# One row-max entry moves from the second to the third attention burst, and score matmuls and row maxima alternate there

## The chip, the cores and the metric

The kernel runs on one core of a Trainium2 chip. The metric is the device time of one execution in microseconds (us), as the median of several runs. TensorE (PE) multiplies and writes its results into PSUM, which has eight banks of 128 x 512 float32 here; VectorE (DVE) and ScalarE (ACT) read them out of the banks; GpSimd (POOL) works on SBUF; SyncE (SP) and the queues of the other engines issue DMAs.

## What is computed

The input is a sequence of 2048 tokens of width 640. Four layers follow each other, A, B, A, B; each is a layer norm, an attention with 32 heads of width 20, a projection, and a residual sum. Layer A is a linear attention. Layer B cuts the sequence into four segments of 512 tokens; in each segment it adds a causal softmax attention to a read of a memory that the earlier segments have filled:

```
logits = jnp.einsum("bhqd,bhkd->bhqk", qs, ks) * scale + mask
p = _softmax(logits, axis=-1)
a_dot = jnp.einsum("bhqk,bhkd->bhqd", p, vs)
o = g * a_mem + (1.0 - g) * a_dot
```

The softmax needs the maximum of each row of logits before the exponentials are taken. The change touches only the order of work in this softmax attention.

## The kernel before

Everything that is not softmax attention (norms, transposes, projections, linear attention, memory) is called dense work below: it is one stream of steps, written as Python generators. The softmax attention is a second stream. A small planner (`run`) interleaves the two while the program is built, by costs that the steps yield. The order of PE's instructions is the order in which the program is written (`MANUAL = ("PE",)`); the other engines' orders are made by a scheduler when the program is built. Every engine then runs its own list strictly in that order.

Softmax attention works on groups of four heads: 8 groups per segment, 32 per B layer, 64 in all. Each group takes part in three successive rounds, as `new`, `prev` and `old`, and each round has three bursts on PE, the three lists of `STRETCHES`. Between two bursts stands dense work, about one projection step of 15 matmuls (L325 or L311), often with a few transposes (L268). An entry of a burst is (operation, number, age), where age 0 is `new`, 1 is `prev` and 2 is `old`:

- `max` (`row_max`, L687 and L694): PE computes logits with queries on the partitions into two banks (one per head of a pair), and DVE reduces each block to its row maxima, with the mask added. `MAXES` says which blocks: entries 0 and 2 are one block of 512 keys per bank, entries 1 and 3 are 384 + 128, entry 4 is 256 + 256. The four reductions of entry 3 belong to the same group as those of entry 4.
- `split` (L703, L704): DVE turns the group's 16 columns of maxima, `mg`, into two float16 parts, `m`. It needs all five `max` entries of the group.
- `rows` (`max_rows`, L712, L714, L717): PE transposes `m` (L712), ACT copies it, and two DMAs on SP's queue write it as extra rows into the queries' tile `qs`, so that the logits of the next step come out with the maximum subtracted. It is done for `prev` in the first burst of the next round.
- `exp` (`scores`, L729, L733, L740): PE computes logits with keys on the partitions into a bank, ACT takes the exponential (L733), POOL clears the part above the diagonal. Entries 0 to 3 of `EXPS` fill two banks each, so does entry 4.
- `sum` (`weigh`, L756): 32 matmuls that weigh the values. `copy` (L762) takes the result out, `out` (`normalize`, L769 to L782) transposes it on PE and divides on DVE.

In the first burst PE does `exp 4`, `max 0`, `max 1`, then `rows` (L712), then the `sum` entries (L756). L712 stands in front of the 32 L756 and of everything behind them.

All banks come from one pool of eight (`bank`, `bufs=8`). A tile takes the place of an earlier one whose readers are done, as the scheduler sees it when the program is built; on the chip PE then waits at the first matmul into a bank until the last reader of the former tile has ended. Each `max` holds its two banks until DVE has reduced them, each `exp` until ACT has read them.

```
for stretch in STRETCHES:
    for op, k, back in stretch:
        G = (new, prev, old)[back]
        ...
    yield SLOT
```

## Time and profile before

| what | value |
|---|---|
| median of 3 runs | 1830.88 us (1830.0 to 1831.1) |
| profiled execution, its own time | 1833.06 us |
| its span, first to last instruction | 1831.3 us |
| mean granted TensorE clock | 0.995 |
| PE busy | 1713.7 us (94%) |
| DVE busy | 1145.0 us (63%) |
| ACT busy | 911.1 us (50%) |
| POOL busy | 502.5 us (27%) |

A timeline row gives the start, the length, the engine, the source line, the operation, what it writes and reads, the shape, how many equal instructions were merged into the row, and in brackets the idle time before it and what ended that. Matmuls overlap each other, and the length of a matmul row reaches to the modelled end of its last matmul; so the time that PE needs for a piece of work is read from start to start. A row of a table of windows gives the stretch, its length, and the busy time of each engine in it with the number of its instructions. In the table of waits stand the waiting engine, tile and line, who ended the wait, the total in us, how often, and the longest.

Softmax attention lies between about 342 and 975 us and between about 1245 and 1806 us of the span.

### The profile page before, as it was taken

What the parts mean: (1) busy time and instruction counts of PE and PEld (TensorE: products, weight loads), DVE (VectorE), ACT (ScalarE), POOL (GpSimd) and SP (SyncE); (2) the same over time, 40 slices, a digit from 0 to 9 for tenths busy, and PEclk for the clock granted to TensorE, in tenths of its full rate; (3) what the DMA queues carried; (4) which work ended last, traced back from release to release, by engine and by line L of the source; (5) the groups of instructions that cost most, each with busy time, mean ns of one, the idle gap of its engine ahead of it and who ended that gap; (6) DMA issues with size and microseconds to landing.
All of it is one profiled execution on the core that took longest, in us unless ns stands there. A gap on an engine that the chain in (4) does not pass through costs nothing.

```text
span 1831.3 us, 36161 instructions
## 1 busy us (share of the span) xinstructions
PE 1713.7 (94%) x13032; PEld 1070.3 (58%) x13032; DVE 1145.0 (63%) x3890; ACT 911.1 (50%) x1696; POOL 502.5 (27%) x925
## 2 busy tenths in 40 slices
PE   6999999999999999898989999999999989998998
PEld 4666676654664565453556776766546546544555
DVE  7655343677777676766663421527687777777783
ACT  5455433256556545545554433333664665565553
POOL 1534440022122113224344334200221231232231
PEclk9999999999999999999999999999999999999999
DMA  7452443312222332352212112432122222323332
GB/s 254 154 188 92 159 143 99 107 58 93 88 67 86 105 103 76 105 186 71 66 56 87 51 33 91 137 108 99 51 91 92 86 90 91 101 77 100 122 112 87
DMA packets 123307, 185.96 MB, mean 102 GB/s; under 512 B 13676, under 2 KB 85484, under 8 KB 120952
## 3 DMA queue, kind: packets, MB, share of 16 engines
q1 hardware_dynamic: 109416, 137.44, 23.5%
q0 software_dynamic: 4496, 25.23, 3.8%
q10 hardware_dynamic: 9216, 20.98, 3.0%
q8 instruction: 103, 1.69, 0.4%
q14 instruction: 76, 0.62, 0.1%
HBM read 104.41 MB, written 78.64 MB: 100 GB/s over the span
## 4 chain that ended last, share of the span: by engine, by line
PE 75%; DVE 11%; ACT 6%; issue 4%; POOL 2%; DMA 2%; SPq 1%; POOLq 0%; ACTq 0%; DVEq 0%
PE ps L325 33%; PE ps L311 18%; PE ps L756 7%; DVE junk L694 4%; PE ps L268 4%; ACT pe L733 3%; PE ps L370 3%; PE ps L729 3%; PE ps L452 2%; PE ps L687 2%; POOL e L341 1%; PE ps L582 1%; PE ps L769 1%; DVE nat L547 1%; PE ps L574 1%
## 5 line engine op out<-in xcount | busy, mean ns | idle before, releaser
L694 DVE CUSTOM_DVE_ANT_0 junk<-ps,maskw 128x512 bf16<-128x512 f32 (+3 forms) x1024 | 499.5, 488 | 83.2 <-PE ps L687 27.1
L733 ACT ACTIVATE pe<-ps,lsc 128x512 f32<-128x512 f32 x640 | 392.7, 691 | 174.5 <-PE ps L729 171.5
L740 POOL TENSOR_SCALAR_AFFINE_SELECT pe<-pe 128x256 f32<-128x256 f32 (+1 forms) x640 | 233.5, 371 | 677.4 <-ACT pe L733 672.0
L325 PEld LDWEIGHTS <-xT 128*128 128x128 f16 x2880 | 281.7, 99 | 124.1 <-issue 18.6
L325 PEld LDWEIGHTS <-oT 128*128 128x128 f16 x1920 | 187.1, 98 | 79.6 <-issue 7.6
L341 POOL TENSOR_SCALAR e<-e 128x320 f32<-128x320 f32 (+1 forms) x104 | 163.7, 1574 | 163.2 <-ACT e L337 154.4
L756 PE MATMUL ps<-pe,v 128*32 128x512 f32 (+3 forms) x2048 | 155.4, 438 | 13.7 <-ACT pe L733 6.8
L729 PE MATMUL ps<-qs,ks 62*128 62x384 f16 (+3 forms) x1024 | 132.2, 299 | 33.4 <-DVE mg L694 22.4
L325 PE MATMUL ps<-w_Bo,oT 128*128 128x320 f16 x960 | 142.8, 301 | 2.6 <-DVE mg L694 1.4
L325 PE MATMUL ps<-w_Bv,xT 128*128 128x320 f16 x960 | 141.3, 301 | 1.9 <-DVE mg L694 1.9
L325 PE MATMUL ps<-w_Av,xT 128*128 128x320 f16 x960 | 141.2, 305 | 1.6 <-DVE w_Av L234 1.0
L311 PE MATMUL ps<-xT,w_Bq 128*128 128x512 f16 x600 | 139.5, 379 | 1.5 <-DVE mg L694 0.9
L311 PE MATMUL ps<-xT,w_Bk 128*128 128x512 f16 x600 | 139.5, 379 | 0.2 <-DVE xn L391 0.2
L325 PE MATMUL ps<-w_Ao,oT 128*128 128x320 f16 x960 | 139.5, 299 | 0.0
L311 PE MATMUL ps<-xT,w_Aq 128*128 128x512 f16 x600 | 136.0, 379 | 1.3 <-DVE xT L273 0.9
L325 PE MATMUL ps<-w_Ak,xT 128*128 128x320 f16 x960 | 135.6, 299 | 1.4 <-DVE mg L694 1.4
L348 ACT ACTIVATE v<-ps 128x320 f32<-128x320 f32 x128 | 55.4, 436 | 143.2 <-PE ps L325 138.9
L291 POOL TENSOR_TENSOR rs<-rs,mhalf 128x1 f32<-128x1 f32 x64 | 35.3, 551 | 302.6 <-DVE rs L290 302.6
L687 PE MATMUL ps<-ks,qs 60*128 60x512 f16 (+3 forms) x1024 | 108.4, 297 | 5.8 <-ACT pe L733 3.6
L756 PEld LDWEIGHTS ps<-pe,v 128*32 128x32 f32 x2048 | 65.3, 110 | 81.2 <-issue 66.3
L547 DVE SCALAR_TENSOR_TENSOR nat<-ps,nat 128x512 f16<-128x512 f32 x80 | 55.3, 691 | 90.3 <-ACT nat L546 86.4
L546 ACT ACTIVATE nat<-ps 128x512 f16<-128x512 f32 x80 | 48.0, 600 | 105.9 <-PE ps L311 76.3
(151 smaller groups left out, 2240.9 us busy)
## 6 DMA issues: line engine op xcount, KB each, us to landing
x<-xn ACTq DMA_DIRECT2D x48, 320.0 KB
qs<-qd SPq DMA_DIRECT2D x128, 120.0 KB
ks<-kd SPq DMA_DIRECT2D x128, 120.0 KB
xo<-x SPq DMA_DIRECT2D x48, 320.0 KB
pqd<-pq POOLq DMA_DIRECT2D x40, 256.0 KB, 2.5
pqi<-pqd SPq DMA_DIRECT2D x32, 320.0 KB
qd<-nat SPq DMA_DIRECT2D x40, 256.0 KB
kd<-nat SPq DMA_DIRECT2D x40, 256.0 KB
```

What stands on the lines that cost most here:

```text
L268: nc.tensor.transpose(pt[:, (c - c0) * P:(c - c0 + 1) * P], src[:, c * P:(c + 1) * P], self.ident)
L311: nc.tensor.matmul(p, w[:, c, a, t * P:(t + 1) * P], xT[:, c, b, :], start=k == 0, stop=k == 3 * C - 1)
L325: nc.tensor.matmul(p, xT[:, c, a, i * P:(i + 1) * P], w[:, c, b, n * HN:(n + 1) * HN], start=k == 0, stop=k == 3 * C - 1)
L341: nc.gpsimd.tensor_scalar(e, e, 1.0, eps, op0=OP.min, op1=OP.add)
L348: self.nc.scalar.activation(vv[:, n * HB:(n + 1) * HB, :DH], p.rearrange("p (h e) -> p h e", e=DH), AF.Copy, scale=V_SHIFT)
L547: nc.vector.scalar_tensor_tensor(nat[:, 1], p, QK_SHIFT, nat[:, 0], op0=OP.mult, op1=OP.subtract)
L687: nc.tensor.matmul(bs[par][:, a:a + n], qs[r, p, i * P:(i + 1) * P], ks[r, p, :n], start=True, stop=True)
L694: nc.vector.tensor_tensor_reduce(junk[:, :n], bs[par][:, a:a + n], self.maskw[:, SEG - n:], 1.0, NEG, OP.add, OP.max, G["mg"][:, par, p, i ...
L729: nc.tensor.matmul(b[:, a:a + n], ks[r, p, j * P:(j + 1) * P], qs[r, p, j * P:], start=True, stop=True)
L733: nc.scalar.activation(e, b, AF.Exp, scale=self.lsc)
L740: nc.gpsimd.affine_select(d, d, pattern=pat, compare_op=OP.is_ge, fill=0.0, base=0, channel_multiplier=-1)
L756: nc.tensor.matmul(G["pv"][32 * h4:32 * h4 + 32, j * P:], v[j][:, h * E1:h * E1 + 32], G.pop((p, par, j)), start=j == 0, stop=j == 2, skip ...
```

## The change

The table of bursts is changed, and nothing else:

```diff
 STRETCHES = [[("exp", 4, 2), ("max", 0, 0), ("max", 1, 0), ("rows", 0, 1), ("sum", 0, 2), ("sum", 1, 2), ("sum", 3, 2),
               ("sum", 2, 2), ("copy", 0, 2)],
-             [("out", 0, 2), ("max", 2, 0), ("max", 3, 0), ("exp", 0, 1), ("exp", 1, 1)],
-             [("exp", 2, 1), ("exp", 3, 1), ("max", 4, 0), ("split", 0, 0), ("load", 0, 0)]]
+             [("out", 0, 2), ("exp", 0, 1), ("max", 2, 0), ("exp", 1, 1)],
+             [("exp", 2, 1), ("max", 3, 0), ("exp", 3, 1), ("max", 4, 0), ("split", 0, 0), ("load", 0, 0)]]
```

The second burst had nine banks to fill and has seven now; the third had six and has eight. No instruction is added or removed.

PE's order in a second burst, before (the group whose second burst stands at 717.84 us of the trace; each L687 or L729 matmul has a weight load ahead of it, and where "..." stands, the same rows come once more):

```order
L769 MATMUL ps<-ident,oTf 128x128 x4
L687 LDWEIGHTS qs
L687 MATMUL ps<-ks_2739,qs 128x512
...
L687 MATMUL ps<-ks_2739,qs 128x384
...
L687 MATMUL ps<-ks_2739,qs 128x128
...
L729 MATMUL ps<-qs,ks_2738 128x512
...
L268 MATMUL ps<-ident,otok 128x128 x2
```

The same burst in the changed program:

```order
L769 MATMUL ps<-ident,oTf 128x128 x4
L729 LDWEIGHTS ks_2738
L729 MATMUL ps<-qs,ks_2738 128x512
...
L687 MATMUL ps<-ks_2739,qs 128x512
...
L729 MATMUL ps<-qs,ks_2738 128x512
...
L268 MATMUL ps<-ident,otok 128x128 x2
```

The blocks of 384 and 128 left this burst and stand in the next one between two pairs of scores, and the first scores now follow the four L769. The banks are dealt out anew as well. Before, in all but a few second bursts one of the last two scores, and often the first dense bank behind the burst too, took a bank that `max 2` had filled in the same burst. In the changed program no score or maximum of a second burst takes a bank that was filled in the same burst, with one exception; the first dense bank behind the burst was freed by earlier work in 34 of 62 cases, is the first bank of `exp 0` in 26, and that of `out` in 2.

DVE's order around `split` in the same group, before:

```order
L694 ISA junk,mg<-ps,maskw 128x256
L694 ISA mg 128x1
L273 TENSOR_TENSOR oT<-ps,oT 128x3x128
L703 TENSOR_SCALAR m_9084<-mg 128x2x8
L704 SCALAR_TENSOR_TENSOR m_9084<-mg,m_9084 128x2x8
L694 ISA junk,mg<-ps,maskw 128x512
```

In the changed program:

```order
L694 ISA junk,mg<-ps,maskw 128x256
L694 ISA mg 128x1
L703 TENSOR_SCALAR m_9084<-mg 128x2x8
L694 ISA junk,mg<-ps,maskw 128x512
L694 ISA mg 128x1
L704 SCALAR_TENSOR_TENSOR m_9084<-mg,m_9084 128x2x8
```

The scheduler has put the next group's first reduction (the L694 of 128x512) between the two halves of `split`. This is so in 33 of the 64 groups of the changed program, and in 2 of the program before.

## The prediction

> **What bounds the kernel now.** I read the page first, then the waits, then one round of attention in the timeline, then tables of windows over all rounds.

> ```profile
> span 1831.3 us, 36161 instructions
> PE 1713.7 (94%) x13032; PEld 1070.3 (58%) x13032; DVE 1145.0 (63%) x3890; ACT 911.1 (50%) x1696; POOL 502.5 (27%) x925
> PE ps L729 <- DVE mg L694: 22.4, 42, 1.0
> PE ps L756 <- ACT pe L733: 6.8, 17, 0.7
> ```

> PE bounds: its list is fixed and nearly always busy, so each microsecond that it waits is a microsecond of the kernel. The waits show one place again and again: a score (L729) waits for a bank that DVE still reduces (L694). The table counts a wait only from a matmul's modelled end, so it understates; starts tell more. One round:

> ```profile
> 717.84 0.60 PE L769 MATMUL ps<-ident,oTf 128*128 128x128 f32 x4
> 718.38 0.61 PE L687 MATMUL ps<-ks,qs 60*128 60x512 f16 x6
> 718.82 1.10 PE L729 MATMUL ps<-qs,ks 62*128 62x512 f16 x4
> 719.30 2.42 ACT L733 ACTIVATE pe<-ps,lsc 128x512 f32<-128x512 f32 x4 [0.81 <-PE ps L729]
> 719.64 0.69 DVE L694 CUSTOM_DVE_ANT_0 junk<-ps,maskw 128x512 bf16<-128x512 f32 x1
> 720.40 0.44 PE L268 MATMUL ps<-ident,otok 128*128 128x128 f32 x2 [0.47 <-DVE mg L694]
> 720.66 0.55 DVE L694 CUSTOM_DVE_ANT_0 junk<-ps,maskw 128x384 bf16<-128x384 f32 x1
> 722.30 0.29 DVE L694 CUSTOM_DVE_ANT_0 junk<-ps,maskw 128x128 bf16<-128x128 f32 x1
> 722.81 0.61 PE L729 MATMUL ps<-qs,ks 62*128 62x384 f16 x8
> 723.25 0.39 PE L687 MATMUL ps<-ks,qs 60*128 60x256 f16 x4
> 723.57 0.55 PE L268 MATMUL ps<-ident,otok 128*128 128x128 f32 x3
> 723.67 0.42 DVE L694 CUSTOM_DVE_ANT_0 junk<-ps,maskw 128x256 bf16<-128x256 f32 x1 [0.74 <-PE ps L687]
> 725.18 0.42 DVE L694 CUSTOM_DVE_ANT_0 junk<-ps,maskw 128x256 bf16<-128x256 f32 x1
> 726.09 0.40 PE L729 MATMUL ps<-qs,ks 62*128 62x256 f16 x4
> 726.13 0.56 DVE L273 TENSOR_TENSOR oT<-ps,oT 128x384 f16<-128x384 f32 x1 [0.52 <-ACT oT L272]
> 726.61 0.17 DVE L703 TENSOR_SCALAR m<-mg 128x16 f16<-128x16 f32 x1
> 726.80 0.18 DVE L704 SCALAR_TENSOR_TENSOR m<-mg,m 128x16 f16<-128x16 f32 x1
> 727.03 0.23 PE L712 MATMUL pm<-ident,m 128*32 128x128 f16 x1
> ```

> The second burst begins at 717.84, and dense work goes on at 720.40, 2.56 us later, right after DVE's second reduction of 128x512 has ended (719.64 + 0.69). PE's own work there is much less: 0.54 for `out` (717.84 to 718.38), 0.44 for six L687 (to 718.82), and as much again for four L729, since these have as many columns: 1.42. So 1.1 us is waiting. The third burst (722.81 to 723.57) does not wait, and behind it DVE has its four reductions of 256 and `split` done at 726.98, just in time for L712 at 727.03.

> All second bursts that hold a maximum, from the first L769 to the next dense matmul:

> ```profile
> 387.82:390.38 2.56, 1.95 (x17) 0.74 (x15) 1.80 (x7) 1.60 (x4) 0.29 (x1) 1.00 0.00 0
> ...
> 1781.41:1783.97 2.56, 1.95 (x17) 0.73 (x15) 2.26 (x8) 1.11 (x2) 0.29 (x1) 1.00 0.35 134
> sum 162.95, PE 119.54 PEld 47.64 DVE 130.69 ACT 84.72 POOL 18.64; mean PE 1.99 PEld 0.79 DVE 2.18 ACT 1.41 POOL 0.31
> ```

> Sixty bursts, 162.95 us, 2.72 each. This is the stall that the change can reach.

> **What the second burst becomes.** `max 3` leaves it (0.22 of PE's time) and the banks no longer come round within the burst. PE needs 0.54 for `out` and 0.22 for each of `exp 0`, `max 2` and `exp 1`: 1.20. Where the dense step behind takes a bank freed long before (34 of 62 by the new program), that is all. In the other 28 it takes a bank of the same burst, nearly always that of `exp 0`. Its release: ACT starts 0.48 after the L729 (718.82 to 719.30) and needs about 0.69 for one, so 0.54 + 0.48 + 0.69 = 1.71. With 32 at 1.20 and 28 at 1.71 the sixty take 86 us. I add 10, an estimate: where ACT still has a projection's three reads ahead of it (some eight bursts) `exp 0` is late by a good half microsecond, and a second dense bank may be that of `exp 0` as well. So 96 against 163: **67 us gained**. Bounds: 91 if every burst takes 1.20; 49 if dense work always waits till 1.9, as it would with ACT a little behind everywhere.

> **What the third burst and L712 become.** DVE has the same reductions to do, but four of them start one burst later. Before, `max 3` was reduced under the dense step between the bursts (720.66 to 722.59); now it comes behind the third burst's scores, and `max 4` and `split` queue behind it on DVE. And PE's next fixed point, L712, needs `split`.

> In this round, counted from the first L729 of the third burst (722.81): the first matmuls of `max 3` start 0.22 later (eight L729 took 0.44), their result reaches DVE 0.42 after that (723.25 to 723.67): 0.64. Four reductions of `max 3` take 1.93 and about 2.01 to the next start; so do the four of `max 4` (723.67 to 725.60). The turn L273 between them adds 0.48 net of overlap. L703 to L712 takes 0.42 (726.61 to 727.03). Sum 5.56. And in this group a reduction of 128x512 now stands between L703 and L704. What that costs, the one kind of group that had it before shows:

> ```profile
> 696.30 0.17 DVE L703 TENSOR_SCALAR m<-mg 128x16 f16<-128x16 f32 x1
> 696.37 0.15 DVE L290 TENSOR_SCALAR rs<-mv 128x1 f32<-128x1 f32 x1
> 696.44 0.68 DVE L694 CUSTOM_DVE_ANT_0 junk<-ps,maskw 128x512 bf16<-128x512 f32 x1
> 697.04 0.17 DVE L704 SCALAR_TENSOR_TENSOR m<-mg,m 128x16 f16<-128x16 f32 x1
> 697.27 0.23 PE L712 MATMUL pm<-ident,m 128*32 128x128 f16 x1 [1.24 <-DVE m L704]
> ```

> L703 to L704 is 0.74 there against 0.19: 0.55 more. So L712 comes 6.1 us after the third burst's start, against 4.22 before: +1.9, and +2.4 if L273 still waits for ACT by 0.52. PE itself would have been there about 0.45 later than before (0.22 for the moved matmuls, as much for a dense bank that is now that of `exp 2`), so this wait, not PE's work, ends last. Queued behind L712 on PE are the 32 L756 and all that follows. Net in this round: +1.9 - 1.36 (2.56 to 1.20), some 0.5 us lost.

> The other groups go by the same arithmetic with their own rows: the time from the third burst to L712 is in these windows, and what DVE has in its list between `max 3` and `split` is read from the new program, at the mean durations of the trace.

> ```profile
> 392.78:396.45 3.67, 3.67 (x38) 2.23 (x37) 2.50 (x12) 3.46 (x7) 1.63 (x4) 1.00 0.00 0
> ...
> 666.70:676.50 9.80, 8.82 (x77) 6.56 (x76) 8.59 (x32) 4.90 (x9) 1.62 (x4) 1.00 0.01 2
> ...
> 1786.49:1790.47 3.98, 3.57 (x34) 2.18 (x33) 3.12 (x14) 3.02 (x6) 1.63 (x4) 1.00 0.00 0
> sum 420.14, PE 393.06 PEld 236.13 DVE 291.10 ACT 291.82 POOL 122.57; mean PE 6.14 PEld 3.69 DVE 4.55 ACT 4.56 POOL 1.92
> ```

> Three classes come out. In 33 groups, mostly with short windows like 3.67, the 128x512 stands in `split`: 69 us in all, 2.0 the median. In 15 without it DVE's chain still ends last: 17 us. In 16 with long windows like 9.80 PE's own path ends last, and only its few tenths are added: 6 us. Sum **92 us lost**. Bounds: 107 if a turn waits for ACT by 0.5 in thirty groups; 50 if little more than half of it appears, because DVE starts each chain earlier than I place it (it is busy only 291 of these 420 us).

> **Given back.** While L712 waits, ACT's exponentials for the L756 behind it get ready; of the 6.8 us that L756 waits for them I take 6 as gone. Other instructions only change place; ACT, POOL and the DMA queues get no more work.

> **Sum.** 92 - 67 - 6 = +19 us. The profiled execution took 1833.06, which would become 1852; against the median of 1830.88, which is 2.2 below it, **1850 us**. The two large terms cancel for the most part: it breaks even where L712 is late by 73 / 62 = 1.2 us a group instead of 1.5.

> **Rivals.** *Faster.* The stall of the second burst goes and DVE catches up. For it: DVE is busy 63% overall, and its idle 0.74 before the first 256 would be filled. Against it: in-order queueing of 2 us of work ahead of `split`, with PE there only 3.7 to 4.2 us after the burst in half of the groups. With half the delay at L712 it is 46 - 67 - 6 = -27; with none, PE's own 0.45 in 60 groups leaves 27 - 67 - 6 = -46. About 1800, chance 0.28. [...]

> *No change.* The terms meet: 79 at L712, a little less than computed, against 73. 1831, chance 0.12.

> *Slower by more.* `exp 0` now opens the second burst 0.44 earlier, and it needs the rows that L712 began, through ACT and two DMAs.

> ```profile
> PEld L729 <- DMA qs<-mt: 5.3, 5, 2.9
> ```

> Five waits show that the slack is sometimes nil. Were it nil everywhere, 0.44 in 60 groups adds 26: 1876. Against it: only five. Decisive once the DMA lands later than the four L769 end. Chance 0.10.

> That the change does not do what it says is excluded by the program's order.

> **Numbers.** My forecast has 0.50. A measurement of this kernel tells about 0.2%, 3.7 us, from no change: slower by more 0.60, within 0.12, faster by more 0.28. The slower cases by themselves span 1837 to 1885; the unknown terms reach from 50 - 91 - 6 = -47 to 107 - 49 = +58. Leaving a tenth out at each end, 1805 to 1880.

> **What would show it.** Second bursts: 1.2 or 1.7 us from L769 to the next dense matmul, sum near 96, no wait of L729 for `mg` there. Third burst to L712: 5.5 to 6.5 in most groups, sum near 512, and L712 at the head of PE's waits, for L704. Wrong if L712 keeps its place: then time falls. Wrong in the other way if the second bursts stay above 2 us because ACT is late.

## The result

| | before | after |
|---|---|---|
| median | 1830.99 us (1830.0 to 1831.92, 4 runs) | 1880.77 us (1877.15 to 1882.77, 4 runs) |
| ratio | | 1.027, 95% interval 1.0252 to 1.0288 |
| profiled execution: time, span | 1833.06, 1831.3 us | 1882.77, 1881.1 us |
| mean granted TensorE clock | 0.995 | 0.986 |

The change makes the kernel 2.7% slower: 50 us, where I had forecast 19. The page and the waits of PE after the change:

```profile
span 1881.1 us, 36046 instructions
PE 1723.2 (92%) x13032; PEld 1076.3 (57%) x13032; DVE 1150.8 (61%) x3890; ACT 913.5 (49%) x1696; POOL 501.9 (27%) x925
...
PE pm L712 <- DVE m L704: 62.4, 42, 2.8
...
PE ps L687 <- ACT pe L733: 10.3, 33, 0.7
PE ps L268 <- ACT pe L733: 9.2, 24, 1.6
...
PE ps L756 <- ACT pe L733: 3.3, 9, 0.6
```

Two of these rows in the kernel before:

```profile
PE pm L712 <- DVE m L704: 6.0, 9, 1.2
PE ps L687 <- ACT pe L733: 3.6, 8, 0.8
```

The wait of L729 for `mg` (22.4 us) is gone, and L712's wait for the second half of `split` has grown from 6.0 us to 62.4. The same round in the timeline after the change:

```profile
734.45 0.60 PE L769 MATMUL ps<-ident,oTf 128*128 128x128 f32 x4
...
735.73 0.44 PE L268 MATMUL ps<-ident,otok 128*128 128x128 f32 x2
...
738.33 0.40 PE L729 MATMUL ps<-qs,ks 62*128 62x384 f16 x4
...
738.98 0.56 DVE L694 CUSTOM_DVE_ANT_0 junk<-ps,maskw 128x384 bf16<-128x384 f32 x1 [0.37 <-PE ps L687]
...
741.07 0.42 DVE L694 CUSTOM_DVE_ANT_0 junk<-ps,maskw 128x256 bf16<-128x256 f32 x1
...
743.52 0.43 DVE L703 TENSOR_SCALAR m<-mg 128x16 f16<-128x16 f32 x1
743.86 0.68 DVE L694 CUSTOM_DVE_ANT_0 junk<-ps,maskw 128x512 bf16<-128x512 f32 x1
744.47 0.16 DVE L704 SCALAR_TENSOR_TENSOR m<-mg,m 128x16 f16<-128x16 f32 x1
744.69 0.23 PE L712 MATMUL pm<-ident,m 128*32 128x128 f16 x1 [1.59 <-DVE m L704]
```

The second burst now takes 1.28 us to the next dense matmul (734.45 to 735.73) where it took 2.56. From the third burst's first matmul to L712 it is 6.36 us where it was 4.22: `max 3` is reduced from 738.98, `max 4` from 741.07, and the next group's 128x512 stands between L703 and L704, which lie 0.95 apart. I had worked out 6.1 for this round.

Over all rounds, from the tables of windows (second bursts first, then third burst to L712; the row of 677.04 is the group that stood at 666.70 before):

```profile
sum 94.74, PE 81.17 PEld 35.85 DVE 61.49 ACT 42.54 POOL 2.30; mean PE 1.35 PEld 0.60 DVE 1.02 ACT 0.71 POOL 0.04
```

```profile
392.24:397.87 5.63, 4.02 (x43) 2.47 (x42) 4.61 (x21) 4.50 (x8) 2.21 (x6) 1.00 0.10 27
...
677.04:689.82 12.78, 11.02 (x80) 7.92 (x79) 10.47 (x41) 4.81 (x9) 1.62 (x4) 0.87 0.01 1
...
sum 541.95, PE 437.79 PEld 254.85 DVE 419.15 ACT 342.28 POOL 163.87; mean PE 6.84 PEld 3.98 DVE 6.55 ACT 5.35 POOL 2.56
```

| stretch | before | after | difference | predicted |
|---|---|---|---|---|
| second bursts (60) | 163.0 | 94.7 | -68.2 | -67 |
| third burst to L712 (64) | 420.1 | 541.9 | +121.8 | +92 |
| L712 to the next dense matmul (62) | 168.3 | 166.1 | -2.1 | -6 |
| sum | | | +51.5 | +19 |

The three stretches account for the difference of the spans (49.8) to within 2 us. The gain came out as computed. The loss came out 30 us larger.

One thing more stands in the trace, and none of my terms had it. The granted clock falls to half for stretches of 3.4 us. Behind the first 30 us of the span there are 5 of these before the change, 17.1 us together, and after it 14, 51.2 us (one of the 14 is twice as long; one more, which begins 2 us before the span ends, isn't counted). PE loses at most half of that time, so this is up to 17 us of the loss. The mean clock agrees: 0.986 against 0.995 over some 1880 us is 17 us. One of them, as two windows of the changed kernel (the seventh column, behind the busy times, is the granted clock) and the timeline of PE at the seam between them:

```profile
534.20:537.60 3.40, 1.28 (x14) 0.63 (x12) 3.26 (x17) 2.83 (x5) 1.36 (x3) 1.00 0.42 109
537.70:541.10 3.40, 3.40 (x29) 1.39 (x33) 2.35 (x10) 0.27 (x1) 0.00 (x0) 0.51 0.11 33
```

```profile
537.62 0.29 PE L712 MATMUL pm<-ident,m 128*32 128x128 f16 x1 [2.13 <-DVE m L704]
537.63 4.06 PE L756 MATMUL ps<-pe,v 128*32 128x512 f32 x32
```

L712 waits 2.13 us, PE is busy for 1.28 of the 3.40 us, and in the next 3.4 us the 32 L756 run at half clock, 4.06 us for all of them. So a stall at L712 seemed to be paid twice, once as a wait and once as a slow stretch behind it. That was a reading of one trace; the experiment with idle transposes tests it.

### The profile page after: what moved, and what is told of

Read it like the earlier page. It is cut to its first block, busy times and chain, and to the rows that moved or that the text cites. A ratio compares the mean times of both kernels' runs of the same rounds, so it can differ in the third digit from the quotient of the medians.

```text
span 1881.1 us, 36046 instructions
## 1 busy us (share of the span) xinstructions
PE 1723.2 (92%) x13032; PEld 1076.3 (57%) x13032; DVE 1150.8 (61%) x3890; ACT 913.5 (49%) x1696; POOL 501.9 (27%) x925
## 4 chain that ended last, share of the span: by engine, by line
PE 71%; DVE 13%; ACT 6%; issue 4%; DMA 3%; POOL 3%; SPq 1%; POOLq 0%; ACTq 0%; DVEq 0%
PE ps L325 29%; PE ps L311 18%; PE ps L756 7%; DVE junk L694 5%; ACT pe L733 4%; PE ps L729 3%; PE ps L268 3%; PE ps L370 3%; PE ps L452 2%; PE ps L687 1%; POOL e L341 1%; PE ps L769 1%; PE ps L582 1%; DVE xn L391 1%; DMA qs<-mt 1%
## 5 line engine op out<-in xcount | busy, mean ns | idle before, releaser
L694 DVE CUSTOM_DVE_ANT_0 junk<-ps,maskw 128x512 bf16<-128x512 f32 (+3 forms) x1024 | 498.8, 487 | 80.1 <-PE ps L687 21.2
L733 ACT ACTIVATE pe<-ps,lsc 128x512 f32<-128x512 f32 x640 | 392.3, 692 | 159.9 <-PE ps L729 141.4
L325 PEld LDWEIGHTS <-xT 128*128 128x128 f16 x2880 | 280.6, 98 | 121.7 <-issue 15.6
L325 PEld LDWEIGHTS <-oT 128*128 128x128 f16 x1920 | 188.5, 99 | 82.6 <-issue 7.5
L756 PE MATMUL ps<-pe,v 128*32 128x512 f32 (+3 forms) x2048 | 163.3, 457 | 6.8 <-ACT pe L733 3.3
L687 PE MATMUL ps<-ks,qs 60*128 60x512 f16 (+3 forms) x1024 | 128.3, 298 | 23.6 <-ACT pe L733 10.3
L325 PE MATMUL ps<-w_Bo,oT 128*128 128x320 f16 x960 | 144.5, 304 | 2.3 <-ACT pe L733 1.4
L325 PE MATMUL ps<-w_Av,xT 128*128 128x320 f16 x960 | 141.1, 305 | 2.2 <-DVE w_Av L234 1.0
L325 PE MATMUL ps<-w_Ao,oT 128*128 128x320 f16 x960 | 141.7, 302 | 0.3
L325 PE MATMUL ps<-w_Bv,xT 128*128 128x320 f16 x960 | 140.0, 299 | 1.4 <-ACT pe L733 0.7
L729 PE MATMUL ps<-qs,ks 62*128 62x384 f16 (+3 forms) x1024 | 132.2, 300 | 9.5 <-DMA qs<-mt 3.9
L325 PE MATMUL ps<-w_Ak,xT 128*128 128x320 f16 x960 | 135.6, 299 | 0.2 <-ACT pe L733 0.2
L756 PEld LDWEIGHTS ps<-pe,v 128*32 128x32 f32 x2048 | 66.9, 114 | 77.0 <-issue 65.0
L273 DVE TENSOR_TENSOR xT<-ps,xT 128x384 f16<-128x384 f32 (+1 forms) x128 | 59.8, 483 | 74.1 <-ACT xT L272 73.6
```

The costliest lines, as they stand in the source:

```text
L273: nc.vector.tensor_tensor(dst[:, c0:c1, 1, i * P:(i + 1) * P], v, hi, op=OP.subtract)
L325: nc.tensor.matmul(p, xT[:, c, a, i * P:(i + 1) * P], w[:, c, b, n * HN:(n + 1) * HN], start=k == 0, stop=k == 3 * C - 1)
L687: nc.tensor.matmul(bs[par][:, a:a + n], qs[r, p, i * P:(i + 1) * P], ks[r, p, :n], start=True, stop=True)
L694: nc.vector.tensor_tensor_reduce(junk[:, :n], bs[par][:, a:a + n], self.maskw[:, SEG - n:], 1.0, NEG, OP.add, OP.max, G["mg"][:, par, p, i ...
L729: nc.tensor.matmul(b[:, a:a + n], ks[r, p, j * P:(j + 1) * P], qs[r, p, j * P:], start=True, stop=True)
L733: nc.scalar.activation(e, b, AF.Exp, scale=self.lsc)
```

## The experiments

The theory to test (**DVE's queue**): L712 is late because `max 3` now stands directly ahead of `max 4` and `split` in DVE's list, with no burst between. Its rivals: the alternation in the third burst makes PE wait for banks; the clock makes up the loss; the way of the rows behind L712 does. All ratios are against the kernel before on the same chip.

**The move without the alternation.**

```
 [("out", 0, 2), ("max", 2, 0), ("exp", 0, 1), ("exp", 1, 1)],
 [("exp", 2, 1), ("exp", 3, 1), ("max", 3, 0), ("max", 4, 0), ("split", 0, 0), ("load", 0, 0)]
```

> The move without the alternation: the second burst is out, max 2, exp 0, exp 1; the third is exp 2, exp 3, max 3, max 4. Theory (DVE's queue): L712 waits for split behind the eight reductions that now all start after the third burst, so the third burst to L712 stays near the 542 us of the changed kernel or grows by the 0.22 us that max 3 starts later (some 10 us over 48 groups); the second bursts, which no longer need a ninth bank, stay near 95 to 105 us. Time 1880 to 1900 us. Rival (alternation in the third burst): the loss is PE's wait for banks between exponentials and maxima, so without it the third burst to L712 falls to about 515 us and the time to some 1855 us.

Measured: 1898.45 us, ratio 1.0366 (1.0337 to 1.0395). Second bursts 93.6 us, third burst to L712 550.8. The first of PE's waits in this kernel:

```profile
PE pm L712 <- DVE m L704: 73.2, 45, 3.4
```

As the theory had it. The alternation in the third burst isn't the loss; with it the kernel is 18 us faster. And the second bursts don't need it: taking `max 3` out frees them by itself.

**The alternation without the move.**

```
 [("out", 0, 2), ("exp", 0, 1), ("max", 2, 0), ("exp", 1, 1), ("max", 3, 0)],
 [("exp", 2, 1), ("exp", 3, 1), ("max", 4, 0), ("split", 0, 0), ("load", 0, 0)]
```

> The alternation without the move: the second burst is out, exp 0, max 2, exp 1, max 3; the third is exp 2, exp 3, max 4 as before the change. Theory (DVE's queue): L712 keeps its old place (third burst to L712 near 420 to 430 us); the second burst still needs a ninth bank, but the one that it comes round to is no longer behind max 2's reductions alone, so it lies between 95 and 163 us, and the time between 1765 and 1831 us, about 1800 us. Rival (alternation costs by itself): the alternation makes PE wait for ACT as often as for DVE, the second bursts stay at 163 us or more, and the time is 1831 us or above.

Measured: 1825.02 us, ratio 0.9962 (0.9949 to 0.9975). Second bursts 145.8 us, third burst to L712 432.7. From PE's waits:

```profile
PE ps L687 <- ACT pe L733: 25.8, 71, 1.2
PE pm L712 <- DVE m L704: 5.8, 11, 1.1
```

L712 keeps its place. The second burst still comes round to a bank of its own, which is now one that ACT reads. It gets back 17 of the 68 us, and 12.5 come back as a longer way from the third burst to L712. So alternation alone is worth 0.4%. I had guessed 1800.

**`split` put ahead.** A scheduling priority was set around L703 and L704.

```
+        with self.tc.high_priority():
             nc.vector.tensor_scalar(m2[:, :, 0], mg, ...)
             nc.vector.scalar_tensor_tensor(m2[:, :, 1], mg, ...)
```

> The changed kernel with the two instructions of split (L703, L704) given precedence, so that no 128x512 reduction stands between them on DVE. Theory (DVE's queue): L712 comes some 0.5 us earlier in the 33 groups that had one there, 15 to 18 us in all, so about 1865 us; the reduction that is put behind must then not make another consumer late. Rival (bank waits of the third burst, or the clock): L712's wait is not what ends last, and the time stays at 1881 us within 4 us.

Measured: 1881.40 us, ratio 1.0273 (1.0235 to 1.031). Not a test: DVE's order came out the same as in the changed kernel, instruction for instruction. It is a second measurement of that kernel, and says only that 1881 repeats. So what the 128x512 within `split` costs has no run of its own. The starts of L703 and L704 lie 25.8 us apart in all groups together before the change and 36.2 after it, which puts it near 10 of the 122 us, an estimate from the two traces.

**`max 3` in the first burst.** The move in the other direction.

```
               ("sum", 2, 2), ("copy", 0, 2), ("max", 3, 0)],
 [("out", 0, 2), ("exp", 0, 1), ("max", 2, 0), ("exp", 1, 1)],
 [("exp", 2, 1), ("exp", 3, 1), ("max", 4, 0), ("split", 0, 0), ("load", 0, 0)]
```

> max 3 at the end of the first burst (behind the copy) instead of in the third; second burst as in the changed kernel, third as before the change. Theory (DVE's queue): the second bursts keep their gain of 68 us, and L712 has only max 4 ahead of it, so the third burst to L712 goes back to some 420 us; the first burst grows by 0.2 us for two banks more (some 13 us). Time about 1775 us. Rival (DVE has no room earlier): max 3's reductions now stand ahead of the transposes' turns and of max 2, so the dense step between the first and the second burst or the second burst waits for banks, 1 us a round, and the time is 1831 us or more.

Measured: 1788.81 us, ratio 0.9770 (0.9747 to 0.9792). L712's row of PE's waits, and the sums of the two tables of windows (second bursts, then third burst to L712):

```profile
PE pm L712 <- DVE m L704: 5.6, 9, 1.0
```

```profile
sum 96.80, PE 84.34 PEld 36.11 DVE 78.33 ACT 44.56 POOL 3.78; mean PE 1.41 PEld 0.60 DVE 1.31 ACT 0.74 POOL 0.06
```

```profile
sum 418.24, PE 392.54 PEld 235.63 DVE 288.18 ACT 297.76 POOL 136.18; mean PE 6.13 PEld 3.68 DVE 4.50 ACT 4.65 POOL 2.13
```

The second bursts keep 66 of the 68 us, L712 is back at its old place, and 19 us go into the longer first burst. The half-clock time is 10.2 us. DVE has room for `max 3` one burst earlier, and none one burst later.

**`max 3` without its reductions.** Left out of the changed kernel: DVE's four reductions of `max 3`, so the row maxima of two row blocks are not computed (zeros stand in their place).

```
-            for p, i, a in todo:
+            for p, i, a in todo if todo is not MAXES[3] else ():
```

> The changed kernel without DVE's four reductions of max 3 (their matmuls stay; the row maxima of two row blocks are zeros instead, so that part of the computation is left out). Theory (DVE's queue): the chain ahead of split is 2 us shorter, L712 comes as early as before the change (third burst to L712 back from 542 to some 430 us), and the half-clock stretches in its wake go too: time near the 1789 us of the kernel with max 3 in the first burst. Rival (PE's third burst itself: two banks and eight matmuls more, and exponentials between them): only the waits on DVE go, the third burst keeps its 128 us, and the time is 1830 us or more.

Measured: 1787.40 us, ratio 0.9757 (0.9736 to 0.9777). L712's row of the waits, and the sum from third burst to L712:

```profile
PE pm L712 <- DVE m L704: 6.5, 10, 1.2
```

```profile
sum 441.54, PE 412.70 PEld 247.34 DVE 293.61 ACT 301.21 POOL 138.80; mean PE 6.45 PEld 3.86 DVE 4.59 ACT 4.71 POOL 2.17
```

Of the 122 us, 100 go with the 2 us of reductions a group (some 10 of them as half clock, which falls from 24.3 us to 3.4 within these stretches); PE's matmuls, the exponentials and their order in the third burst are all still there. What stays, 21 us, is about the growth of the third bursts themselves that is left: from their first matmul to the next dense one, the 64 took 65.2 us before the change and take 89.1 here, where the change has 117.9. The half-clock time is back at 17.1 us.

**Idle transposes in L712's wait.** As many as the wait of the changed kernel holds, group by group: 771 in 42 groups. They write to columns of L712's bank that nothing reads. The code in plain form:

```
+        for k in range(FILL[n]):      # n: the group's number; FILL: 6 to 28, or 0
+            nc.tensor.transpose(pt[:, P * (1 + k % 7):P * (2 + k % 7)], self.ident16, self.ident16)
         nc.tensor.transpose(pt[:32, :P], m2.rearrange("q a k r -> q (a k r)"), self.ident16)
```

> The changed kernel with 771 idle transposes (128x128, f16) put on TensorE right ahead of L712, 6 to 28 of them in each of the 42 groups in which it waits for split, as many as fit into the wait. They work on the bank that L712 writes and nothing reads them. Theory (clock): stretches of 3.4 us in which PE is under about half busy are followed by a stretch at half clock; with PE kept busy in the wait those after L712's waits do not come, the half-clock time falls from 51 us to some 20 us, and the time falls by 8 to 15 us to about 1868 us although PE has more to do. Rival (the clock does not follow PE's idle time, or half clock costs nothing there): the same number of half-clock stretches, and the time stays at 1881 us or rises by the transposes that do not fit.

Measured: 1870.07 us, ratio 1.0208 (1.0190 to 1.0227), against 1.0252 to 1.0288 without them. Half-clock time 20.5 us in place of 51.2. The same seam as above, as PE's timeline and as windows of this kernel (the transposes are the line L707):

```profile
534.58 1.72 PE L707 MATMUL pm<-ident 128*128 128x128 f16 x28 [0.31 <-ACT pe L733]
536.41 0.23 PE L712 MATMUL pm<-ident,m 128*32 128x128 f16 x1
536.42 2.37 PE L756 MATMUL ps<-pe,v 128*32 128x512 f32 x32
```

```profile
532.90:536.30 3.40, 3.09 (x43) 2.36 (x41) 3.29 (x17) 2.83 (x5) 1.37 (x3) 1.00 0.38 108
536.30:539.70 3.40, 3.29 (x41) 1.67 (x42) 2.48 (x11) 0.86 (x2) 0.00 (x0) 1.00 0.16 44
```

L712 starts hardly earlier in its group (third burst to L712 is 538.8 us in all), the clock stays at 1.00, and the 32 L756 take 2.37 us in place of 4.06. From L712 to the next dense matmul the rounds now take 155.6 us in place of 166.1. The kernel does more and is 11 us faster. So filling the stall takes the half clock behind it away, and that second payment is 11 us or somewhat more. The theory's "under about half busy" is an estimate from windows like that of 534.20 us (busy for 1.28 of 3.40 us); over the whole changed kernel half clock follows ten of the thirteen stretches that were busy 0.50 or less, and five that were busier, up to 0.73.

**L712 two steps later.** The step `rows` behind the first two `sum` entries.

```
-  ("max", 1, 0), ("rows", 0, 1), ("sum", 0, 2), ("sum", 1, 2), ("sum", 3, 2),
+  ("max", 1, 0), ("sum", 0, 2), ("sum", 1, 2), ("rows", 0, 1), ("sum", 3, 2),
```

> The changed kernel with the step that holds L712 two steps later in the first burst, behind the first two of the four sums (L756), so about 0.9 to 1.2 us of PE work stands ahead of it. Theory (DVE's queue): L712's wait shrinks by that much in some 45 groups, 40 to 50 us in all, and its wait for DVE falls from 62 to some 20 us; time about 1835 us. Rival (the rows' way behind L712 is as tight as the wait ahead of it): the rows come later to qs by the same amount, L729 in the second burst waits for the DMA instead, and the time stays at 1881 us within 10 us.

Measured: 1819.85 us, ratio 0.9933 (0.9910 to 0.9955): 61 us less than the changed kernel, and below the kernel before. From PE's waits:

```profile
PE ps L729 <- DMA qs<-mt: 7.1, 2, 3.6
PE pm L712 <- DVE m L704: 4.1, 6, 1.4
```

DVE does the same in nearly the same order (96 of its 3890 places differ, and the 128x512 stands within `split` in the same number of groups, 33), and `split` is as late as it was: from the start of the third burst to its end a median of 6.56 us, and 6.57 in the changed kernel. PE has something else to do meanwhile. 58 of the 62 us of waiting are gone, and with them more than half of the half-clock time (23.9 us are left). The second bursts pay 6 us.

**L712 behind all four sums.** As the last, but with `rows` behind the fourth `sum`.

> The changed kernel with the step that holds L712 behind all four sums in the first burst (two steps later than in the run with the rows behind two sums). Theory (DVE's queue, with the rows' way as its other end): L712 has no wait left to lose (4.1 us), so nothing is gained beyond 1820 us, and the rows reach qs about 1 us later, so L729 waits for the DMA in many more than 2 rounds: 1820 to 1880 us, slower than with the rows behind two sums. Rival (only L712's wait matters): 1820 us or less.

Measured: 1833.88 us, ratio 1.0016 (1.0003 to 1.0029). The first of PE's waits:

```profile
PE ps L729 <- DMA qs<-mt: 18.7, 32, 5.2
```

Here is the other end. L712 waits hardly any more for `split` (2.0 us), the rows are late for `exp 0` in 32 rounds, and the second bursts grow to 121.4 us, from 101.2 in the run before this one. My rival of the rows' DMA is real, but it decides only when L712 stands a microsecond later than in the run before this one; in the changed kernel this wait is 3.9 us.

**`max 3` at the head of the third burst.**

```
-  [("exp", 2, 1), ("max", 3, 0), ("exp", 3, 1), ("max", 4, 0), ...
+  [("max", 3, 0), ("exp", 2, 1), ("exp", 3, 1), ("max", 4, 0), ...
```

> The changed kernel with its third burst in the order max 3, exp 2, exp 3, max 4, so that DVE can begin 0.2 us earlier and no maximum stands between exponentials. Theory (DVE's queue): L712 comes 0.2 us earlier in 48 groups, some 10 us, so about 1871 us; the waits of L687 for ACT's banks (10 us) go or move to the dense step behind. Rival (order of banks in the third burst decides): the time falls by 25 us or more, to 1855 us or less.

Measured: 1855.50 us, ratio 1.0135 (1.0114 to 1.0156). From PE's waits:

```profile
PE pm L712 <- DVE m L704: 39.9, 34, 2.5
PE ps L687 <- ACT pe L733: 10.8, 24, 0.7
```

The time is the rival's, its mechanism is not: the waits of L687 for ACT add up to as much as they did (10.3). The third burst to L712 falls by 26 us to 515.9. The first reduction behind the burst starts 0.29 us earlier on average (0.22 in the median), and DVE's list changed in its order too, so that L703 and L704 lie 26.2 us apart in all, not 36.2: a 128x512 stands between them in 15 groups, not in 33, which the run with the priority was meant to try. The half-clock time falls to 27.3 us. I had counted the first of these only. How much each is worth this run doesn't separate.

**More on top of the first-burst version.** Three kernels side by side: that version again; with `max 4` ahead of `exp 3`; with `rows` behind the first `sum`.

> The kernel with max 3 at the end of the first burst again, beside the two that build on it. Theory (DVE's queue): 1789 us again, within 3 us. Rival (a chance of the earlier comparison): above 1800 us.

> max 3 at the end of the first burst and, beside that, the third burst as exp 2, max 4, exp 3. Theory (DVE's queue): max 4 reaches DVE 0.2 us earlier, but L712 waits only 9 times for DVE there (5.6 us in all), so no more than 3 us are gained: 1784 to 1790 us. Rival (order of banks in the third burst): the dense step behind takes a bank that ACT still reads, as in the changed kernel (L268 for L733, 9.2 us against 4.9), and the time rises by 3 to 10 us.

> max 3 at the end of the first burst and, beside that, the step that holds L712 one step later, behind the first sum. Theory (DVE's queue): L712's waits there are 5.6 us for DVE and 2.7 us for ACT; most of that goes, and the time falls by 3 to 8 us to about 1783 us. Rival (the rows' way): L729 in the second burst waits for the DMA in more rounds, and nothing is gained or 5 us are lost.

Measured: 1787.70 (0.9750 to 0.9781), 1788.78 (0.9752 to 0.9783) and 1786.17 us (0.9741 to 0.9775). The three can't be told apart. With `rows` later, L712's wait for `split` (5.6 us) goes, and the second bursts grow from 96.9 to 108.0 us. The version to keep is `max 3` in the first burst: 2.3% faster than the kernel before, 5% faster than the change.

## Why the prediction was right or wrong

**The stall of the second burst: right.** 68.2 us against 67. I had 32 bursts at 1.20 us and 28 at 1.71; 31 took about 1.3, 26 took 1.6 to 1.85, and three took longer. The 10 us that I added are luck in part: not some eight bursts were late by half a microsecond, but one took 4.94 us, and the short ones 0.09 more than I had. The two alone-runs add whose it is: the whole of it comes from taking `max 3` out.

**What is late next: right in place and cause.** L712 heads PE's waits, for L704, as written. Without the reductions of `max 3` 100 of its 122 us vanish, and with other work ahead of L712 the wait vanishes though DVE is as late as in the changed kernel.

**The size of that term: wrong, 92 against 122.** By the prediction's three classes:

| class | groups | predicted | measured |
|---|---|---|---|
| 128x512 within `split` | 33 | 69 | 78 |
| DVE's chain without it | 15 | 17 | 20 |
| "PE's own path ends last, and only its few tenths are added" | 16 | 6 | 24 |

The step that failed is the last: 18 of the 30 us that are missing lie there. I took a long window for a safe one. The group of 666.70 us shows why it isn't. Its PE before the change:

```profile
667.59 0.39 PE L687 MATMUL ps<-ks,qs 60*128 60x256 f16 x3 [0.17 <-DVE oa L381]
...
669.91 0.60 PE L574 MATMUL ps<-ident,pkT 128*128 128x128 f32 x4
670.35 2.20 PE L325 MATMUL ps<-w_Ao,oT 128*128 128x320 f16 x15
```

and after it:

```profile
678.19 0.39 PE L729 MATMUL ps<-qs,ks 62*128 62x384 f16 x2 [0.32 <-DVE oa L381]
679.52 0.39 PE L687 MATMUL ps<-ks,qs 60*128 60x256 f16 x4 [0.94 <-DVE otok L381]
...
682.09 1.06 PE L574 MATMUL ps<-ident,pkT 128*128 128x128 f32 x4
682.94 2.93 PE L325 MATMUL ps<-w_Ao,oT 128*128 128x320 f16 x15
...
689.82 0.23 PE L712 MATMUL pm<-ident,m 128*32 128x128 f16 x1
```

L712 doesn't wait here. But the burst asks for two banks more, and finds some that dense work's own DVE step (L381) still reads. So PE waits 0.32 + 0.94 us within the burst, where it waited 0.17, and half clock then covers the four L574 (1.06 us; 0.60 before) and the L325 behind them (2.93; 2.20 before). Third burst and clock together, 2.98 us more in a group that I had down for 0.45. In the 16 groups the third bursts grew from 23.1 to 38.0 us, and 13.7 us of half clock fell into their windows (none before), about 6.8 us lost. Without the reductions of `max 3` the third bursts of these groups take 29.2: more than half of their growth goes with DVE's work. My upper bound (107) counted no such path.

**The clock: missing.** I priced every instruction at full clock. In all windows from third burst to L712 half-clock time rose from 3.4 to 24.3 us, which is some 10 of the 30 us that the term came out too small by. Of these 10, 6.8 lie in the 16 groups above and 3.6 in the other two classes. What else made those two 12 us larger than I had them stays open; the waits of L687 for ACT's banks, which none of my terms had, grew from 3.6 to 10.3 us.

**Given back, 6 us: 2.1.** The waits of L756 for ACT fell from 6.8 to 3.3 us, not to nearly nothing. The clock took its part: from L712 to the next dense matmul half-clock time rose from 3.4 to 20.1 us, 8 us lost. Where it is absent, with the idle transposes, this stretch is 12.7 us shorter than before the change.

**The rivals.** "Faster" fell, though each of its halves is real: the second burst's stall does go, and DVE does have room, but a burst earlier. As far as banks go the trace agrees with it (94.7 us for 163.0 in the second bursts); it fell over the consumer that waits for what is taken out of them (L712, 62.4 us). "Slower by more" gave 1876, close to the result, for the wrong reason: L729 waits only 3.9 us for the rows. "No change" had a slip: 79 against 73 is 6 us lost, so 1837 by its own numbers and not 1831.

**The range** ended at 1880 and the result is 1880.8. Its upper bound was made of the terms that I had; two terms were missing, and both had one sign.

## What to carry to other kernels

When an operation is moved past a burst, look for the consumer at the end of the queue that it joins: here 2 us of reductions moved from under a dense step to directly ahead of `split`, and freed banks in one burst were worth a little over half of what the next fixed point lost. Where such a consumer can't be served earlier, put other work of the waiting engine ahead of it (61 us here), or move the operation the other way (92 us). And a stall can be paid a second time in clock: here the 2.13 us ahead of one L712 were followed by 3.4 us at half clock.

## What the runs showed of the hardware

| kernel | L712 waits for `split`, us | half clock, us |
|---|---|---|
| before | 6.0 | 17.1 |
| change | 62.4 | 51.2 |
| move only | 73.2 | 51.2 |
| `max 3` at the head | 39.9 | 27.3 |
| change, L712 two steps later | 4.1 | 23.9 |
| change, L712 behind all four sums | 2.0 | 34.1 |
| change, idle transposes | 10.3 | 20.5 |
| no reductions of `max 3` | 6.5 | 17.1 |
| `max 3` in the first burst | 5.6 | 10.2 |

At the L712 of 537.62 us a wait of 2.13 us, in a stretch of 3.40 us in which PE was busy for 1.28, was followed by half clock. What decides between a stretch that is followed by one and a stretch that isn't, these runs don't settle.
